# A linear-attention and gated-MLP kernel on one core: two heads of the attention share a pair of PSUM banks and one operation, and small vector work moves to GpSimd

## The chip, the cores and the metric

The kernel runs on one core of one Trainium2 chip. The metric is the device time of one execution in microseconds. Over three runs the kernel before took 1269.21 us at the median (1263.41 to 1276.26).

## The reference

What is computed is a linear attention over 8 batches, 8 heads, 576 tokens and a head size of 64, with 128 random features, and behind it a gated layer over the 4608 tokens (512 model columns, 1536 inner columns):

```python
def phi(x):                                   # x: q or k, already scaled by 64 ** -0.25
    proj = np.einsum('bhsd,md->bhsm', x, omega)
    sq = np.sum(x * x, axis=-1, keepdims=True) / 2.0
    h = proj - sq
    h = h - np.max(h, axis=-1, keepdims=True)
    return np.exp(h) / np.sqrt(m)
q_p, k_p = phi(q_s), phi(k_s)
kv = np.einsum('bhsm,bhsd->bhmd', k_p, v)
z = np.sum(k_p, axis=2)
out = einsum('bhsm,bhmd->bhsd', q_p, kv) / (einsum('bhsm,bhm->bhs', q_p, z)[..., None] + 1e-6)
x = out, heads side by side: (4608, 512)
gate = 1 / (1 + np.exp(-(x @ w_gate)))
return gate * (x @ w_val) @ w_out
```

The weights of the gated layer come in as 64-bit floats.

## The kernel before, in words

The attention works on "units" of two batches (1152 tokens, nine tiles of 128) and pairs of heads: four units `u`, four pairs `p`, two halves `b` (the two batches). It is written as generators, each a task that yields between its steps: `norms` (row sums of squares of q or k, line 489), `keys` (line 558, up to the tile `kv` of key features times values) and `queries` (line 601). `attention` (line 687) keeps up to six tasks going and steps them in turn.

The steps of one task are a chain through four engines. TensorE projects the tokens onto the features (`pp`, line 527 with each head's 64 rows of the array, in a bank per head, or line 536 for a tile that stands alone, with both heads in one matmul over 128 rows against a zero-padded omega). VectorE takes the maxima (`mx`, line 550), then the small tiles `hm` (line 554) and `nb` (line 573, keys) or `sub` (line 611, queries). For keys, ScalarE takes the exponentials `kp` out of the bank (line 582), and TensorE sums `pkv` (line 592). For queries, VectorE subtracts (`h`, line 617), TensorE transposes (`pt`, line 631), ScalarE takes the exponentials `qp` (line 633), TensorE multiplies with `kv` (`pn`, line 644), VectorE divides (`den`, `inv`, `x`, lines 649 to 654), TensorE transposes back (`px`, line 661), ScalarE copies (`xs`, line 667), and a DMA puts the rows into `xT` in DRAM. From the maxima on, each of these is done once per head.

The gated layer is in three passes. `first_pass` (line 224) makes four of the twelve column tiles from `xT`: products `gv` (line 243) in split single precision, a low and a high word of each operand, so three matmuls for each of four contraction steps, twelve per product. ScalarE takes the tanh of the gate (`ge`, line 264), VectorE multiplies (`ye`, line 271), and a DMA stores. The low words `xe` are subtracted on GpSimd (line 71). The first pass is interleaved with the attention: after each of its steps, `RATE` steps of the attention are recorded (lines 736 to 744), and since a chunk of tokens needs finished attention, `load` (line 215) records attention steps until they are there. `second_pass` (line 391, products `gw`, line 347) and `last` (line 440, products `po`, line 461) follow when the attention is done.

In between, the 64-bit weights are turned into single precision by `from_float64` (line 74): five VectorE operations and one more with the low word (line 94), then an addition on GpSimd (line 96) and subtractions there (line 177). Three of these conversions are left for the stretch after the attention (tiles `late`).

PSUM has eight banks: six with the tag `at` and two with `gv`. While the attention is alone, and again in the second and last pass, `any_bank` (line 124) deals all eight out in turn. While attention and first pass run together, the attention has the six and `gv` the two; after the attention, `gv` still has its two.

The order of the instructions on each engine isn't the order in which they are recorded. A scheduler sets it from its own costs of the operations and from when buffers come free; each engine then runs its list strictly in that order, and waits where an operand or a buffer isn't ready.

## Time and profile before

| what | value |
|---|---|
| median of three runs | 1269.21 us |
| profiled execution, its own time | 1265.23 us |
| its span, first to last instruction | 1263.4 us |
| first `gv` product on TensorE begins | 77.6 us |
| last `px` transpose of the attention begins | 521.9 us |
| first `gw` product of the second pass begins | 613.4 us |
| busy over the span: TensorE, VectorE, ScalarE, GpSimd | 94%, 67%, 38%, 34% |

The program has four stages: attention alone (to 77.5 us), attention with the first pass (to about 522 us), the rest of the first pass (to 613 us), then second and last pass. A view of the profile groups instructions by line, engine and operation: their busy time, the mean of one in ns, and what ended the idle time ahead of them. A busy time is the union of the spans in the group, and the spans of neighbouring matmuls overlap, so the pace of matmuls is read from the distance of their starts. A matmul of 32-bit floats shows as two records in the trace. "PEclk" is the clock granted to TensorE as a share of the full one.

### The profile page before, as it was taken

To read this page: it belongs to the slowest core of one execution; us is meant where nothing else is said; L and a number is where in the kernel's file an instruction comes from. 1 tells how busy PE (TensorE), PEld (TensorE's weight loads), DVE (VectorE), ACT (ScalarE), POOL (GpSimd) and SP (SyncE) were. 2 spreads that over 40 slices of the span, in tenths; PEclk is the share of its full clock that TensorE was granted. 3 is DMA by queue.
4 is the path that set the end of the run, shared out by engine and by line. 5 is a ranking of instruction groups with operands and counts; after the bars stand their busy time and mean duration, and the time that the engine had idled before them with its cause. 6 is when DMAs were issued, how large, how long until landed. Compare 5 with 4: busy or idle time off the path is not lost.

```text
span 1263.4 us, 23711 instructions
## 1 busy us (share of the span) xinstructions
PE 1189.8 (94%) x9052; PEld 1105.9 (88%) x9052; DVE 848.5 (67%) x1842; ACT 474.5 (38%) x971; POOL 431.3 (34%) x439
## 2 busy tenths in 40 slices
PE   7889899989899999987999999999999899999998
PEld 6778888777777887866899999999998899999998
DVE  4678788778847455475566565665668787677773
ACT  3445454534333434322422222322224443343331
POOL 0223041423422001163176666666666211111110
PEclk9679779989989999998999999999999999999999
DMA  7647577766673531456423333233328676666662
GB/s 241 208 159 241 187 239 255 253 212 211 219 244 107 164 97 57 139 206 235 148 88 122 147 125 115 95 122 122 134 85 285 208 223 190 208 193 185 196 186 93
DMA packets 100338, 219.40 MB, mean 174 GB/s; under 512 B 10624, under 2 KB 33408, under 8 KB 98432
## 3 DMA queue, kind: packets, MB, share of 16 engines
q1 hardware_dynamic: 87984, 198.94, 47.6%
q10 hardware_dynamic: 12240, 18.95, 4.2%
q8 instruction: 71, 1.16, 0.4%
q14 instruction: 43, 0.35, 0.1%
HBM read 141.82 MB, written 76.02 MB: 172 GB/s over the span
## 4 chain that ended last, share of the span: by engine, by line
PE 68%; DVE 11%; DMA 7%; issue 7%; POOL 4%; ACT 2%; SPq 1%; ACTq 0%; DVEq 0%; POOLq 0%
PE gw L347 25%; PE po L461 20%; PE gv L243 7%; PE pkv L592 6%; PE pn L644 4%; PE ppk L527 2%; PE pt L631 2%; POOL xe L71 2%; DMA xr<-xT 2%; PE ppq L527 1%; DVE mxk L550 1%; DMA u<-w 1%; DVE mxq L550 1%; DMA xT<-xs 1%; DVE h L617 1%
## 5 line engine op out<-in xcount | busy, mean ns | idle before, releaser
L347 PE MATMUL gw<-xl,u 128*128 128x256 f32 x3024 | 362.6, 282 | 6.1 <-DVE u L327 5.2
L347 PEld LDWEIGHTS gw<-xl,u 128*128 128x128 f32 x3024 | 361.1, 189 | 7.5 <-DVE u L327 6.0
L461 PE MATMUL po<-u,yh 128*128 128x256 f32 x1512 | 272.4, 283 | 0.0
L461 PEld LDWEIGHTS po<-u,yh 128*128 128x128 f32 x1512 | 234.8, 191 | 0.0
L461 PE MATMUL po<-u,yl 128*128 128x256 f32 x756 | 213.9, 283 | 4.0 <-DVE yl L71 4.0
L243 PE MATMUL gv<-xe,wh 128*128 128x512 f32 (+1 forms) x640 | 200.0, 392 | 2.9 <-POOL xe L71 2.8
L70 ACT ACTIVATE yh<-yr 128x896 fp32r<-128x896 f32 x108 | 100.3, 950 | 157.3 <-PE po L461 63.1
L461 PEld LDWEIGHTS po<-u,yl 128*128 128x128 f32 x756 | 144.3, 191 | 4.4 <-DVE yl L71 4.4
L243 PEld LDWEIGHTS gv<-xe,wh 128*128 128x128 f32 x640 | 120.6, 199 | 24.1 <-POOL xe L71 4.6
L243 PE MATMUL gv<-xe,wl 128*128 128x512 f32 (+1 forms) x320 | 128.3, 403 | 13.2 <-DVE ye L271 10.3
L71 DVE TENSOR_TENSOR yl<-yr,yh 128x896 fp32r<-128x896 f32 x91 | 101.1, 1123 | 37.0 <-PE po L461 23.1
L71 POOL TENSOR_TENSOR yl<-yr,yh 128x896 fp32r<-128x896 f32 x17 | 38.2, 2249 | 215.6 <-PE po L461 139.5
L71 POOL TENSOR_TENSOR xe<-xr,xe 128x512 fp32r<-128x512 f32 (+1 forms) x40 | 49.5, 1251 | 172.7 <-ACT xe L70 164.8
L592 PE MATMUL pkv<-v,kp 128*128 128x66 f32 x512 | 88.4, 308 | 13.9 <-ACT kp L582 13.8
L592 PEld LDWEIGHTS pkv<-v,kp 128*128 128x128 f32 x512 | 80.4, 222 | 22.6 <-ACT kp L582 19.2
L327 DVE TENSOR_TENSOR u<-gw,p 128x256 f32<-128x256 f32 x144 | 60.7, 422 | 58.7 <-PE gw L347 50.8
L243 PEld LDWEIGHTS gv<-xe,wl 128*128 128x128 f32 x320 | 63.7, 200 | 26.6 <-DVE ye L271 12.1
L96 POOL TENSOR_TENSOR c<-c 128x512 f32<-128x512 f32 x22 | 28.2, 1283 | 165.5 <-DVE c L94 91.0
L452 DVE TENSOR_TENSOR yr<-yr 128x128 f32<-128x128 f32 x144 | 64.4, 482 | 28.1 <-DMA yr<-ye 27.5
L644 PE MATMUL pn<-kv,qp 128*128 128x66 f32 (+1 forms) x640 | 75.5, 273 | 3.1 <-DVE h L617 3.1
L644 PEld LDWEIGHTS pn<-kv,qp 128*128 128x128 f32 (+1 forms) x640 | 70.4, 189 | 8.2 <-DVE h L617 3.5
L633 ACT ACTIVATE qp<-pt 128x512 f32<-128x512 f32 (+1 forms) x80 | 43.6, 555 | 89.1 <-PE pt L631 85.9
(106 smaller groups left out, 1776.9 us busy)
## 6 DMA issues: line engine op xcount, KB each, us to landing
yl<-yl SPq DMA_DIRECT2D x36, 896.0 KB, 3.8
yr<-yl SPq DMA_DIRECT2D x72, 448.0 KB, 4.0
xr<-xT SPq DMA_DIRECT2D x68, 256.0 KB, 4.4
c<-w SPq DMA_DIRECT2D x22, 512.0 KB, 4.9
w<-c SPq DMA_DIRECT2D x11, 1024.0 KB, 4.9
v<-va SPq DMA_DIRECT2D x32, 330.0 KB, 3.5
natk<-kn SPq DMA_DIRECT2D x36, 256.0 KB, 4.1
natq<-qn SPq DMA_DIRECT2D x36, 256.0 KB, 4.0
```

The costliest lines, as they stand in the source:

```text
L70: nc.scalar.activation(out=hi, in_=x, func=AF.Copy)
L71: (lo_engine or nc.vector).tensor_tensor(out=lo, in0=x, in1=hi.bitcast(F32), op=ALU.subtract)
L96: nc.gpsimd.tensor_tensor(out=x, in0=x, in1=r, op=ALU.add)
L243: nc.tensor.matmul(gv, lhsT=u[:, s], rhs=v, start=(m == 0), stop=(m == 3 * KC - 1))
L327: return nc.vector.tensor_tensor(out=o, in0=a, in1=b, op=ALU.add)
L347: nc.tensor.matmul(o, lhsT=u[:, k, s], rhs=v[:, kc, :], start=(first and m == 0), stop=(m == 5), skip_group_check=not first,)
L452: nc.vector.tensor_tensor(out=raw[:, o], in0=raw[:, a], in1=raw[:, b], op=op)
L461: nc.tensor.matmul(o, lhsT=u[:, i, :], rhs=v[:, k, :], start=(j + m == 0 and n in (1, 6, 5, 4)), stop=(j == NPAIR - 1 and m == 2), skip_gr ...
L527: nc.tensor.matmul(pps[h][:, i * M : (i + 1) * M], lhsT=raw[r, (t - t0) * P : (t - t0 + 1) * P], rhs=om_sb[r, h * M : (h + 1) * M], start= ...
L592: nc.tensor.matmul(pkv[:, h, :], lhsT=kp[b * MID + i, h], rhs=v[:, i, h, :], start=(i == 0), stop=(i == MID),)
L633: nc.scalar.activation(out=qp, in_=pt, func=AF.Exp)
L644: nc.tensor.matmul(pn[r, i, :], lhsT=qp[:, i, r], rhs=kvs[u, p, bb][:, h, :], start=True, stop=True,)
```

## The change

- Every projection takes both heads together: a tile of two banks `[128, 2, 512]`, head 0 in the first and head 1 in the second, and from there one operation for both heads: maxima, `h`, the exponentials of the queries, the division. The six `at` banks become three such pairs. The form with a zero-padded omega is gone; a tile that stood alone is now in a group with others (`GROUPS`: keys 0-2 and 3-4, then 5-8; queries 0-3, then 4-6 and 7-8).
- Omega is scaled once (`om_s`), so that `h` is an addition with `nb`. `hm` and `nb` are subtractions on GpSimd (lines 549 and 552 of the changed kernel).
- The squares come scaled from ScalarE, GpSimd adds the two halves of each head (`half`, line 510), and VectorE sums 32 values a head (line 511) in place of 64. The eight sums have buffers of their own.
- In `from_float64` the low word is scaled on ScalarE (line 94) and multiplied on GpSimd (line 95).
- The first chunk is 512 tokens, not two of 256, and the attention alone ends when 512 tokens are through (a group of queries makes 512 at once). `RATE` is 9 for 12, `FROM` 16 for 24; some buffer counts differ.
- After the attention, `gv` is dealt out over all eight banks. While the attention is alone, `pkv` and `px` take a `gv` bank, later one half of a pair.

The core of the diff:

```diff
-GROUPS = {"k": (((0, 1, 2, 3), (4,)), ((5, 6, 7, 8),)), "q": (((0, 1, 2, 3),), ((4,), (5, 6, 7, 8)))}
+GROUPS = {"k": (((0, 1, 2), (3, 4)), ((5, 6, 7, 8),)), "q": (((0, 1, 2, 3),), ((4, 5, 6), (7, 8)))}
...
-FROM = 24
+FROM = 16
...
-RATE = 12
-RAWS, KPS, VS, HS, XS = 6, 8, 3, 5, 3
+RATE = 9
+RAWS, KPS, VS, HS, XS = 6, 14, 3, 3, 2
...
-    nc.vector.scalar_tensor_tensor(out=r, in0=lo, scalar=2.0**-52, in1=r, op0=ALU.mult, op1=ALU.mult)
+    nc.scalar.activation(out=small, in_=lo, func=AF.Copy, scale=2.0**-52)
+    nc.gpsimd.tensor_tensor(out=r, in0=small, in1=r, op=ALU.mult)
     nc.gpsimd.tensor_tensor(out=x, in0=x, in1=r, op=ALU.add)
...
+    def two_banks(name):
+        return pairs.tile([P, 2, 512], F32, tag="at", bufs=3, name=name)
+    def one_bank(name):
+        return bank(name) if alone else two_banks(name)[:, 0]
...
-            gv = bank("gv", f"gv{o}_{j}_{i}")[:, :n]
+            gv = (any_bank if late else bank)(f"gv{o}_{j}_{i}")[:, :n]
...
-        chunks = [(0, Q), (Q, Q)] + [(c * NC, NC) for c in range(1, NCH)]
+        chunks = [(c * NC, NC) for c in range(NCH)]
...
-            nc.scalar.activation(out=x2, in_=x, func=AF.Square)
+            nc.scalar.activation(out=x2, in_=x, func=AF.Square, scale=SCALE / 2.0**0.5)
             yield
-            nc.vector.tensor_reduce(
-                out=s[:, t - t0, :], in_=x2.rearrange("p (h d) -> p h d", d=D), axis=AX.X, op=ALU.add
-            )
+            nc.gpsimd.tensor_tensor(out=half, in0=x2[:, :, 0], in1=x2[:, :, 1], op=ALU.add)
+            nc.vector.tensor_reduce(out=s[:, t - t0, :], in_=half, axis=AX.X, op=ALU.add)
...
-            nc.vector.scalar_tensor_tensor(
-                out=hm, in0=mx[:, i0:i1], scalar=SCALE, in1=s, op0=ALU.mult, op1=ALU.subtract,
-            )
+            nc.gpsimd.tensor_tensor(out=hm, in0=s, in1=mx, op=ALU.subtract)
+            nc.gpsimd.tensor_tensor(out=nb, in0=hm, in1=s, op=ALU.subtract)
...
-                nc.vector.scalar_tensor_tensor(
-                    out=h_sb,
-                    in0=pp,
-                    scalar=SCALE,
...
-                    op0=ALU.mult,
-                    op1=ALU.subtract,
-                )
+            nc.vector.tensor_tensor(
+                out=h_sb, in0=pp, in1=nb.unsqueeze(3).broadcast_to([P, 2, nt, M]), op=ALU.add
+            )
...
-            while not ready(Q):
+            while not ready(NC):
...
-                credit += RATE if n >= 4 * NE else RATE // 2
+                credit += RATE if n >= 2 * NE else RATE // 2
...
+        rest = ctx.enter_context(tc.tile_pool(name="rest", bufs=1, space=bass.MemoryType.PSUM))
+        cycle[:] = ["at", "at", "at", "gv"]
```

What it moves in the lists of the engines is seen at three places. The first is a group of keys, unit 1, pair 2, first half. Before, its maxima (`mxk1_2_0`) and both small tiles (`hmk1_2_0`, `nb1_2_0`) stand on VectorE:

```order
L550 TENSOR_REDUCE mxk1_2_0_1658<-ppk1_2_0_0_1659 128x4
L550 TENSOR_REDUCE mxk1_2_0_1658<-ppk1_2_0_1_1660 128x4
L550 TENSOR_REDUCE mxk1_2_0_1658<-ppk1_2_4_1671 128x2
L649 TENSOR_SCALAR den0_3_5_1_1703<-pn0_3_5_1_1698 128x4
L554 SCALAR_TENSOR_TENSOR hmk1_2_0_1674<-mxk1_2_0_1658,sqk1_0_1343 128x10
L503 TENSOR_SCALAR sqq2_0_3245<-ssq2_0_3038 128x32
L653 RECIPROCAL inv0_3_5_1_1705<-den0_3_5_1_1703 128x4
L573 SCALAR_TENSOR_TENSOR nb1_2_0_1678<-sqk1_0_1343,hmk1_2_0_1674 128x10
```

Now `hm` and `nb` of the same group stand in GpSimd's list. `c3` is a weight conversion, `halfq2_7` the squares of a later unit, `xe512` low words of the first pass:

```order
L510 TENSOR_TENSOR halfq2_7_3549<-x2q2_7_3519 128x256
L95 TENSOR_TENSOR c3_3528<-c3_3528 128x512
L96 TENSOR_TENSOR c3_3528<-c3_3528 128x512
L549 TENSOR_TENSOR hmk1_2_0_1536<-ssk1_0_1042,mxk1_2_0_1521 128x10
L552 TENSOR_TENSOR nbk1_2_0_1538<-hmk1_2_0_1536,ssk1_0_1042 128x10
L71 TENSOR_TENSOR xe512_2_1620<-xr512_0_904,xe512_2_1620 128x512
```

So the small tiles left a list of maxima and divisions and stand behind a multiplication and an addition of 128x512 that wait for the weights' DMA.

The second place is TensorE in a group of queries, unit 2, pairs 0 to 3. Before, each head's four transposes and products are pieces of their own:

```order
L631 MATMUL pt2_0_0_0_3356<-id_sb_69,h2_0_0_0_3311 128x128 x4
L631 MATMUL pt2_1_0_1_3368<-id_sb_69,h2_1_0_1_3269 128x128 x4
L631 MATMUL pt2_2_0_1_3375<-id_sb_69,h2_2_0_1_3291 128x128 x4
L631 MATMUL pt2_0_0_1_3382<-id_sb_69,h2_0_0_1_3313 128x128 x4
L527 MATMUL ppq2_3_0_0_3390<-om_sb_67,rawq2_3_0_3315 128x128
```

Now:

```order
L605 MATMUL pt2_0_0_3158<-id_sb_69,h2_0_0_3103 128x128 x8
L617 MATMUL pn2_1_0_3176<-kv2_1_0_2850,qp2_1_0_3132 128x66 x8
L539 MATMUL ppq2_2_0_3192<-om_s_71,rawq2_2_0_3084 128x128 x8
L617 MATMUL pn2_0_0_3208<-kv2_0_0_2732,qp2_0_0_3167 128x66 x8
L634 MATMUL px2_1_0_3232<-id_sb_69,x2_1_0_3189 128x128 x4
```

Both heads' eight go at once, and each of these rows fills one of the three pairs.

The third place is the end of the attention on TensorE. Before, the last `px` (unit 3, pair 3) stands among the products of the chunk from token 2560, and 319 matmuls `gv` are still to come:

```order
L644 MATMUL pn3_3_5_1_5726<-kv3_3_1_5299,qp3_3_5_1_5706 128x66 x4
L243 MATMUL gv2560_2_0_5868<-xe2560_3_5315,wh2_790 128x512
L243 MATMUL gv2560_2_1_5883<-xe2560_0_5306,wl2_791 128x512
L243 MATMUL gv2560_2_1_5883<-xe2560_0_5306,wh2_790 128x512 x2
L243 MATMUL gv2560_2_1_5883<-xe2560_1_5309,wl2_791 128x512
L243 MATMUL gv2560_2_1_5883<-xe2560_1_5309,wh2_790 128x512
L661 MATMUL px3_3_5_5736<-id_sb_69,x3_3_5_5645 128x128 x4
```

Now it stands among those of the chunk from token 3072, with 250 to come:

```order
L634 MATMUL px3_2_7_5494<-id_sb_69,x3_2_7_5481 128x128 x2
L252 MATMUL gv3072_3_0_5677<-xe3072_0_5304,wl3_891 128x512
L252 MATMUL gv3072_3_0_5677<-xe3072_0_5304,wh3_890 128x512
L634 MATMUL px3_3_7_5523<-id_sb_69,x3_3_7_5492 128x128 x2
L252 MATMUL gv3072_3_0_5677<-xe3072_0_5304,wh3_890 128x512
```

So 69 matmuls of 512 columns moved from behind the attention to within it.

More of the change, by code (lines that the diff above doesn't have):

```diff
@@ L111, in attn_glu_kernel @@
     yl = dram.tile([NPAIR - EP, P, NCH, 2, N_OPS, P], F32, name="yl")
-    om_sb = const.tile([P, 2 * M], F32, name="om_sb")
+    om_sb = const.tile([P, M], F32, name="om_sb")
     nc.sync.dma_start(out=om_sb, in_=om)
@@ L542, in projected @@
             i0, i1 = some[0][0] - t0, some[-1][-1] + 1 - t0
[L543 removed]
+            mx = pool.tile([P, 2, MID + 1], F32, tag="mx", bufs=4, name=f"mx{name}{u}_{p}_{some[0][0]}")[:, :, : i1 - i0]
             pps = []
             for tiles in some:
[L546 to L551 removed]
@@ new lines, in projected @@
+                for i, t in enumerate(tiles):
+                    for h in range(2):
+                        r = slice(h * D, (h + 1) * D)
+                        nc.tensor.matmul(
+                            pp[:, h, i], lhsT=raw[r, (t - t0) * P : (t - t0 + 1) * P], rhs=om_s[r],
+                            start=True, stop=True, skip_group_check=True,
+                        )
+                o = tiles[0] - t0 - i0
+                nc.vector.tensor_reduce(out=mx[:, :, o : o + nt], in_=pp, axis=AX.X, op=ALU.max)
@@ new lines, in queries @@
+            for h in range(2):
+                for i in range(nt):
+                    nc.tensor.transpose(out=pt[:, h, i], in_=h_sb[:, h, i], identity=id_sb)
+            qp = pool.tile([P, 2, nt, P], F32, tag="qp", bufs=HS, name=f"qp{id_}")
+            nc.scalar.activation(out=qp, in_=pt, func=AF.Exp)
+            yield
+            pn = two_banks(f"pn{id_}")[:, :, : nt * E].rearrange("p h (i e) -> p h i e", e=E)
+            for h in range(2):
+                for i, t in enumerate(tiles):
@@ L694, in attention @@
                     i for i, (name, needs, _) in enumerate(tasks[:AHEAD])
-                    if (ready(Q) or name[1] == name[-1] == 0) and done.issuperset(needs) and kinds.count(name[0][0]) < ACTIVE[name[0][0]]
+                    if (ready(NC) or name[1] == name[-1] == 0) and done.issuperset(needs) and kinds.count(name[0][0]) < ACTIVE[name[0][0]]
                 ]
@@ L715, in attn_glu_kernel @@
     late = None
+    alone = True
     stores = []
@@ L718, in attn_glu_kernel @@
         gates = first_pass()
-        with tc.tile_pool(name="a", bufs=1, side="right") as pool:
+        with (
+            tc.tile_pool(name="a", bufs=1, side="right") as pool,
+            tc.tile_pool(name="pairs", bufs=1, space=bass.MemoryType.PSUM) as pairs,
+        ):
             steps = attention(pool)
```

166 lines of the change are left out of this document (58 added, 108 removed).

## The prediction

> **What bounds the kernel now.** I read the page first: busy time per engine, and the clock granted to TensorE over 40 slices of the span.
>
> ```profile
> PE 1189.8 (94%) x9052; PEld 1105.9 (88%) x9052; DVE 848.5 (67%) x1842; ACT 474.5 (38%) x971; POOL 431.3 (34%) x439
> PEclk9679779989989999998999999999999999999999
> ```
>
> TensorE is busy 94% of the time and nothing else is above 67%. But its clock dips, all in the left half. So I took the busy times by stage, in stretches of the span (attention alone, attention with first pass, rest of the first pass, the two later passes). The columns are each engine's busy time, the granted clock, the DMA share and GB/s.
>
> ```profile
> 0.00:77.50 77.50, 60.85 (x358) 52.99 (x358) 47.29 (x117) 32.22 (x79) 10.55 (x13) 0.85 0.64 209
> 77.50:525.00 447.50, 418.04 (x3097) 360.05 (x3096) 317.30 (x820) 192.94 (x507) 106.87 (x103) 0.93 0.56 185
> 525.00:615.00 90.00, 77.32 (x323) 61.23 (x322) 49.70 (x67) 27.28 (x42) 37.43 (x32) 0.94 0.56 195
> 615.00:1263.40 648.40, 633.61 (x5280) 631.64 (x5278) 434.19 (x841) 222.07 (x344) 276.40 (x292) 1.00 0.48 158
> ```
>
> In the last row TensorE lacks 15 us of 648 and has its full clock. The change touches nothing there. The first 615 us hold what can be won: TensorE is idle for 77.5 - 60.9 = 16.7, 29.5 and 12.7 us, and a clock of 0.85, 0.93 and 0.94 costs about 11.6, 31.3 and 5.4 us more. Together that is 107 us of 615; some 508 are work at full clock. VectorE is busy 317 of 447.5 us in the middle, 71%. GpSimd, at 107, has room.
>
> The waits of TensorE say for what: the total, the number of times, and the longest. First in the middle stage, then (last row) behind the attention.
>
> ```profile
> PE pt L631 <- DVE h L617: 11.2, 13, 2.5
> PE pkv L592 <- ACT kp L582: 10.7, 10, 2.3
> PE pn L644 <- DVE h L617: 3.1, 1, 3.1
> PE gv L243 <- DVE ye L271: 10.3, 4, 5.4
> ```
>
> So 25.0 us of the 29.5 are the chain of an attention group being late, from VectorE directly or through the exponentials, and 10.3 of the 12.7 are a bank of `gv` that VectorE has not read yet.
>
> The clock isn't simply a matter of long waits. In this stretch TensorE sat still for 1.06 us of 10 and yet had half its clock:
>
> ```profile
> 150.00:160.00 10.00, 8.94 (x47) 8.31 (x48) 4.94 (x18) 2.45 (x4) 0.00 (x0) 0.50 0.29 85
> ```
>
> The Trainium skill's page "TensorE: Matmul & The Clock Gate" (Part 1) says that the clock halves after an idle window of about 3.4 us and returns after a busy one. This row disagrees: no wait of the middle stage is that long. By the rule the 31 us of lost clock there would not be, and fewer waits would bring nothing on that side; by the rows they are there. I count no gain in clock in the forecast.
>
> **The change, part by part.** *TensorE's own work.* 32 single tiles lose their both-heads matmul. Its place in the trace, start to start: 0.53 us at full clock, against 1.09 us for sixteen records of half-row matmuls.
>
> ```profile
> 136.32 1.16 PE L527 MATMUL ppk<-om_sb,rawk 64*128 64x128 f32 x16
> 137.41 0.70 PE L536 MATMUL ppk<-om_sb,rawk 128*128 128x256 f32 x2
> 137.94 1.04 PE L631 MATMUL pt<-id_sb,h 128*128 128x128 f32 x8
> ```
>
> 32 x 0.53 = 17.0 us go, and 64 half-row matmuls, two records each, come: 128 x 1.09/16 = 8.7 us. That saves 8.3 at full clock, double at half clock; I take 9. The first chunk's 192 matmuls of 256 columns become 96 of 512. Their pace is one low-word matmul to the next, three matmuls apart:
>
> ```profile
> 129.95 0.28 PE L243 MATMUL gv<-xe,wl 128*128 128x256 f32 x1
> 130.31 0.28 PE L243 MATMUL gv<-xe,wl 128*128 128x256 f32 x1
> 599.76 0.39 PE L243 MATMUL gv<-xe,wl 128*128 128x512 f32 x1
> 600.44 0.39 PE L243 MATMUL gv<-xe,wl 128*128 128x512 f32 x1
> ```
>
> 0.36/3 = 0.12 us and 0.68/3 = 0.227 us, so 23.0 becomes 21.8: 1 us. Sum: **-10** (-9 to -18).
>
> *The rest of the first pass.* It lasts from the last `px` to the first `gw`:
>
> ```profile
> 521.92 0.60 PE L661 MATMUL px<-id_sb,x 128*128 128x128 f32 x4
> 613.36 2.92 PE L347 MATMUL gw<-xl,u 128*128 128x256 f32 x23
> ```
>
> From 522.5 to 613.4 are 90.9 us, for 319 matmuls that need 319 x 0.227 = 72.4. The excess is 18.5. Afterwards 250 stand there, 56.8 us; the other 69 (15.7 us) are done earlier, which moves work and saves none. What saves is that `gv` gets eight banks, so four gates and values, 8 x 12 x 0.227 = 21.8 us of products, may lie between TensorE and a late `ye`. The longest wait in the row above is 5.4 us. I expect those 10.3 us to go. What is late next is the preparation of the second pass, since VectorE's 49.7 and GpSimd's 37.4 us of this stage now have 65 us in place of 91, and GpSimd gets the six multiplications of the late weights, 6 x 1.28 = 7.7 us. I keep 7.5 of the excess: **-11** (bounds -18.5 and 0, where the whole excess stays because VectorE is late everywhere).
>
> *VectorE's load.* One operation for both heads saves only the fixed part of an operation. The spans of the maxima and of `h` by size (shortest, median, longest) give it:
>
> ```profile
> L550 DVE TENSOR_REDUCE mxq<-ppq x80: 415/684/703, 34.3 to 513.1; 128x4 f32<-128x512 f32 x64, 128x2 f32<-128x256 f32 x16
> L617 DVE SCALAR_TENSOR_TENSOR h<-ppq,sub x80: 409/681/694, 40.9 to 515.7; 128x512 f32<-128x512 f32 x64, 128x256 f32<-128x256 f32 x16
> L653 DVE RECIPROCAL inv<-den 128x4 f32<-128x4 f32 (+1 forms) x80 | 13.0, 168 | 0.6
> L649 DVE TENSOR_SCALAR den<-pn 128x4 f32<-128x4 f32 (+1 forms) x80 | 12.7, 159 | 53.0 <-PE pn L644 52.3
> L611 DVE TENSOR_TENSOR sub<-sqq,hmq 128x8 f32<-128x8 f32 (+1 forms) x48 | 13.1, 274 | 0.2
> L554 DVE SCALAR_TENSOR_TENSOR hmq<-mxq,sqq 128x8 f32<-128x8 f32 (+1 forms) x48 | 10.0, 209 | 0.2
> L554 DVE SCALAR_TENSOR_TENSOR hmk<-mxk,sqk 128x10 f32<-128x10 f32 (+1 forms) x32 | 7.9, 251 | 0.3
> L573 DVE SCALAR_TENSOR_TENSOR nb<-sqk,hmk 128x10 f32<-128x10 f32 (+1 forms) x32 | 9.6, 303 | 0.2
> L499 DVE TENSOR_REDUCE ssq<-x2q 128x8 f32<-128x512 f32 x36 | 24.2, 679 | 0.5 <-ACT x2q L497 0.5
> L94 DVE SCALAR_TENSOR_TENSOR c<-c 128x512 f32<-128x512 uint32 x22 | 15.5, 703 | 0.3
> ```
>
> 256 elements take 0.415 us and 512 take 0.684: 1.05 ns an element and 0.146 us fixed. 160 maxima become 96 (48 groups of queries, 48 of keys), 64 x 0.146 = 9.3 us; `h` and `x` go from 80 to 48, 2 x 32 x 0.14 = 9.0; `den` and `inv` likewise, 32 x 0.327 = 10.5. `sub`, `hm` and `nb` leave: 13.1 + 10.0 + 7.9 + 9.6 = 40.6. The sums of squares lose 256 of 512 elements, 72 x 256 x 1.05 ns = 19.4. The low words leave: 36 x 0.703 = 25.3. Altogether 114 us, about 100 of them in the middle, where VectorE falls from 71% to 48%.
>
> *GpSimd's load.* It gets 72 halves of 256, 36 multiplications of 512 and 160 tiny subtractions. Nearest rows:
>
> ```profile
> L384 POOL TENSOR_TENSOR yl<-gl,yl 128x256 f32<-128x256 f32 x36 | 27.7, 770 | 2.2 <-DVE gl L382 2.2
> L96 POOL TENSOR_TENSOR c<-c 128x512 f32<-128x512 f32 x22 | 28.2, 1283 | 165.5 <-DVE c L94 91.0
> L874 POOL MEMSET const-float32-1.0<- 128x1 f32 x1 | 0.1, 98 | 0.0
> ```
>
> 0.770 and 1.283 us put 0.26 us at zero elements. No tiny subtraction is in the trace: it costs between the 0.098 of setting one element and the 0.770 of 256; I take 0.27, by the line through the two sizes. Then 72 x 0.77 + 36 x 1.28 + 160 x 0.27 = 145 us (117 to 225), some 125 in the middle: 107 becomes 232 of about 450 us, 52%. The multiplication reads its low word at a stride, which no GpSimd row shows; at worst twice the price, 46 us more. The page "GPSIMD Engine Reference" of the Trainium skill (section 4.1) speaks against this: elementwise work belongs on VectorE, GpSimd being about twice as slow. The rows agree, 1.283 against 0.703 us for neighbouring steps; but as an engine with time to spare pays, the sum doesn't change. ScalarE gets 36 copies of the size of this one, 36 x 0.634 = 23 us, at 193 busy of 447.5, and only GpSimd waits for them:
>
> ```profile
> L70 ACT ACTIVATE wh<-e 128x512 fp32r<-128x512 f32 x8 | 5.1, 634 | 10.2 <-POOL e L96 10.2
> ```
>
> There is a second cost. The same step of a weight conversion, in the middle and behind the attention, where GpSimd was busier (37.4 of 90 us):
>
> ```profile
> L85 DVE TENSOR_SCALAR c<-c 128x512 uint32<-128x512 uint32 x22 | 11.5, 523 | 0.2
> L85 DVE TENSOR_SCALAR late<-late 128x512 uint32<-128x512 uint32 x6 | 4.8, 821 | 0.1
> ```
>
> This step loses 0.30 us. If all five steps of the 30 conversions in the attention did, that would be 45 of the 100 us saved; VectorE still ends below 60%.
>
> *The waits of the middle.* The 25.0 us are a group's chain being late. Its VectorE part gets less queueing. Its GpSimd part is new: two dependent operations, 0.54 us, behind whatever stands ahead of them, in 80 groups. And the banks get scarcer: three pairs serve where six banks did, and a `pkv` or a `px` now takes a whole pair. I take the two as nearly even and count **-6** for waits, +-25.
>
> **The sum:** -10 - 11 - 6 = -27 us from the profiled execution's 1265.2 (its span of 1263.4 and 1.8 around it, which stay), so 1238. The median of the runs shown, 1269.2, is 0.3% above that execution; I forecast 1240.
>
> **Rivals.** *TensorE keeps its clock* (about 1210). If the groups' chains shorten as VectorE's load does, by a third or more, the waits fall to 12 us in place of 25, and of the 43 us of clock lost up to 525 us a third returns: -10 - 11 - 13 - 14 = -48, so 1217 from the profiled execution, or with the whole excess behind the attention gone 1209. For it: the half-clock stretches lie where groups are late. Against it: the row of 150 to 160, half clock with little idle time.
>
> *Nothing comes of VectorE's relief* (about 1262). It was at 71% and nobody's bound; GpSimd takes the place in the chain, and the eight banks only move the wait into the second pass's start. Then -10 from TensorE's work remain and some 7 us of new waits against them: 1265 - 10 + 7. For it: TensorE is at 93 to 94% already in the middle.
>
> *Slower: the small tiles stand behind the weights on GpSimd* (about 1290). GpSimd's list puts `hm` and `nb` of a group behind a multiplication and an addition of a conversion, which wait for the weights' DMA and five VectorE steps. Meanwhile a group of keys holds two of the three pairs, the other tasks share one, and TensorE, in order, stops at `pkv` or `pt`. There are 30 such conversion halves in the attention, 2 x 1.28 = 2.6 us each on GpSimd: 77 us if all is exposed. It decides from 0.9 us exposed per half (30 x 0.9 = 27); at two thirds, 51 us, the time is 1265 - 27 + 51 = 1289. The page "SBUF — State Buffer" of the Trainium skill (Who interferes with whom) adds that a GpSimd instruction and a VectorE one that needs their shared port block each other fully; the two rows of line 85 above agree with it (523 against 821 ns), and it would lengthen this chain further. Against it: `gv` products fill TensorE's list between the groups, and 0.9 us is more than the mean queue that 52% makes.
>
> **How the numbers follow.** The forecast, 1223 to 1256: 0.45. The clock kept, below 1223: 0.21. Nothing gained, 1256 to 1282: 0.17. Slower: 0.17. A change of 1%, 12.7 us, is about what a measurement can tell here. So faster 0.66, the same 0.17, slower 0.17. The range of 1205 to 1284 leaves out a little below and about a tenth above.
>
> **What would show it.** Right: the first `gw` starts near 587 us where it stood at 613; the wait of `gv` for `ye` is gone; VectorE in the middle is near 50% and GpSimd near 50%; TensorE's waits there are about 20 us, and some now name GpSimd or exponentials behind it. Wrong: if TensorE waits over 50 us in the middle for `kp` and `h` behind GpSimd's `nb`, the slower rival holds; if the tiny subtractions take over 0.5 us, my price of the chain was too low; if the clock row changes by much either way, I erred in leaving it out.

## The result, and the profile after

The changed kernel takes 1323.1 us at the median (four runs, 1319.24 to 1326.8) beside 1269.21 us for the kernel before in the same session: ratio 1.042 (95% interval 1.034 to 1.050). Some executions are in a slower state (one of the kernel before took 1864 us), and all medians and ratios here leave them out. The changed kernel is slower, by some 54 us. The prediction, 1240 us and most likely faster, was wrong.

The profiled execution took 1319.24 us, with a span of 1317.4. The page's busy times, and the clock over 40 slices:

```profile
PE 1212.5 (92%) x9020; PEld 1114.7 (85%) x9020; DVE 786.8 (60%) x1434; ACT 490.1 (37%) x968; POOL 564.0 (43%) x703
PEclk9988866998799999899979999999999999999999
```

VectorE lost 62 us of work, GpSimd gained 133, and TensorE, with 32 records fewer, is busy for longer. By stage, with the columns of the prediction's table (attention alone, attention with first pass, rest of the first pass, the later passes):

```profile
0.00:79.70 79.70, 62.75 (x353) 55.72 (x354) 40.92 (x69) 36.00 (x83) 34.39 (x50) 1.00 0.61 202
79.70:591.40 511.70, 451.56 (x3129) 374.91 (x3128) 264.19 (x466) 204.93 (x499) 211.45 (x328) 0.88 0.50 165
591.40:650.30 58.90, 57.75 (x249) 46.32 (x248) 35.31 (x42) 16.48 (x26) 38.06 (x32) 1.00 0.53 190
650.30:1317.40 667.10, 640.41 (x5293) 637.75 (x5291) 446.37 (x857) 232.70 (x360) 280.08 (x294) 0.98 0.48 161
```

The attention ends at 591 where it ended at 522.5. The moved `gv` work is 69 matmuls or 15.7 us of that, so about 53 us are lost ahead of it. In the middle TensorE is idle for 511.7 - 451.6 = 60.1 us, where it was 29.5, and its clock is 0.88 where it was 0.93. The rest of the first pass is 59 us in place of 91, but the last stage has grown by 17 us. Its first 50 us, in the kernel before and in the changed one:

```profile
613.40:663.40 50.00, 47.24 (x390) 46.63 (x389) 33.73 (x64) 19.11 (x33) 26.96 (x31) 1.00 0.39 137
```

```profile
650.30:700.30 50.00, 35.08 (x247) 33.99 (x246) 34.11 (x55) 24.44 (x38) 19.07 (x18) 0.76 0.61 210
```

247 matmuls fit in where 390 did. TensorE's waits over the whole span, the two longest rows and three of `gw` (total, number of times, longest):

```profile
PE pkv L580 <- ACT kp L571: 20.9, 10, 10.3
PE pt L605 <- DVE h L598: 20.8, 15, 5.8
PE gw L356 <- ACT xl L298: 8.1, 1, 8.1
...
PE gw L356 <- ACT p L367: 4.4, 1, 4.4
PE gw L356 <- DVE u L336: 4.1, 4, 1.4
```

Behind `kp` and `h` stands GpSimd. This is what ScalarE and VectorE waited for:

```profile
ACT kp L571 <- POOL nbk L552: 58.3, 23, 6.4
```

```profile
DVE h L598 <- POOL nbq L552: 30.1, 38, 4.2
```

One piece of the timeline shows how the lists hang together (ScalarE, GpSimd, VectorE and TensorE, start and duration; in brackets the idle time ahead and what ended it):

```profile
118.88 1.29 POOL L95 TENSOR_TENSOR c<-c 128x512 f32<-128x512 f32 x1 [1.75 <-DVE c L92]
120.13 0.72 POOL L510 TENSOR_TENSOR halfk<-x2k 128x256 f32<-128x256 f32 x1
120.80 1.26 POOL L96 TENSOR_TENSOR c<-c 128x512 f32<-128x512 f32 x1
...
122.70 3.13 POOL L186 TENSOR_TENSOR c<-c 128x256 f32<-128x256 f32 x4
...
125.79 0.71 POOL L510 TENSOR_TENSOR halfk<-x2k 128x256 f32<-128x256 f32 x1
...
126.54 0.42 DVE L511 TENSOR_REDUCE ssk<-halfk 128x8 f32<-128x256 f32 x1 [1.29 <-POOL halfk L510]
126.75 0.21 POOL L552 TENSOR_TENSOR nbk<-hmk,ssk 128x8 f32<-128x8 f32 x1
...
126.99 1.14 ACT L571 ACTIVATE kp<-ppk,nbk 128x128 f32<-128x128 f32 x4 [3.58 <-DVE ssk L511]
...
127.41 0.69 PE L580 MATMUL pkv<-v,kp 128*128 128x66 f32 x2 [10.29 <-ACT kp L571]
```

GpSimd works without a pause from 118.9 to 126.9, but on a conversion and on halves. VectorE's sum waits for a half that stands behind the conversion, `nb` comes at 126.75, and TensorE has stood still for 10.3 us. It looks like the prediction's slower rival. The experiments show that this is only part of it.

### The profile page after: what moved, and what is told of

The parts are those of the page before. It is cut to its first block, busy times and chain, and to the rows that moved or that the text cites. A ratio compares the mean times of both kernels' runs of the same rounds, so it can differ in the third digit from the quotient of the medians.

```text
span 1317.4 us, 23526 instructions
## 1 busy us (share of the span) xinstructions
PE 1212.5 (92%) x9020; PEld 1114.7 (85%) x9020; DVE 786.8 (60%) x1434; ACT 490.1 (37%) x968; POOL 564.0 (43%) x703
## 4 chain that ended last, share of the span: by engine, by line
PE 45%; DVE 3%; DMA 1%; issue 1%; SPq 0%; POOL 0%; ACT 0%; DVEq 0%; ACTq 0%; POOLq 0%
PE gw L356 26%; PE po L470 19%; DMA u<-w 1%; DVE u L221 1%; DMA yr<-ye 1%; DVE yr L461 0%; DVE yl L71 0%; SPq L443 0%; POOL late L186 0%; DVE u L336 0%; DVE o L336 0%; DVE ye L280 0%; DVE yl L336 0%; DVE u L215 0%; DVE gl L336 0%
## 5 line engine op out<-in xcount | busy, mean ns | idle before, releaser
L356 PE MATMUL gw<-xl,u 128*128 128x256 f32 x3024 | 367.6, 284 | 18.2 <-ACT xl L298 8.1
L252 PE MATMUL gv<-xe,wh 128*128 128x512 f32 x576 | 199.0, 421 | 3.2 <-POOL xe L71 3.1
L252 PEld LDWEIGHTS gv<-xe,wh 128*128 128x128 f32 x576 | 112.5, 200 | 27.9 <-POOL xe L71 5.6
L252 PE MATMUL gv<-xe,wl 128*128 128x512 f32 x288 | 124.3, 434 | 9.0 <-ACT xe L70 6.2
L571 ACT ACTIVATE kp<-ppk,nbk 128x128 f32<-128x128 f32 x256 | 69.4, 387 | 61.9 <-POOL nbk L552 58.3
L617 PEld LDWEIGHTS pn<-kv,qp 128*128 128x128 f32 (+1 forms) x640 | 77.4, 199 | 17.2 <-issue 5.7
L617 PE MATMUL pn<-kv,qp 128*128 128x66 f32 (+1 forms) x640 | 85.2, 292 | 6.6 <-DVE x L627 3.1
L544 DVE TENSOR_REDUCE mxk<-ppk 128x6 f32<-128x768 f32 (+2 forms) x48 | 44.7, 952 | 60.4 <-PE ppk L539 60.1
L252 PEld LDWEIGHTS gv<-xe,wl 128*128 128x128 f32 x288 | 57.0, 199 | 21.0 <-ACT xe L70 6.4
L71 POOL TENSOR_TENSOR xe<-xr,xe 128x512 fp32r<-128x512 f32 x36 | 48.3, 1350 | 58.6 <-ACT xe L70 58.6
```

The costliest lines, as they stand in the source:

```text
L71: (lo_engine or nc.vector).tensor_tensor(out=lo, in0=x, in1=hi.bitcast(F32), op=ALU.subtract)
L252: nc.tensor.matmul(gv, lhsT=u[:, s], rhs=v, start=(m == 0), stop=(m == 3 * KC - 1))
L356: nc.tensor.matmul(o, lhsT=u[:, k, s], rhs=v[:, kc, :], start=(first and m == 0), stop=(m == 5), skip_group_check=not first,)
L544: nc.vector.tensor_reduce(out=mx[:, :, o : o + nt], in_=pp, axis=AX.X, op=ALU.max)
L571: nc.scalar.activation(out=kp[t][:, h], in_=pp[:, h, i], func=AF.Exp, bias=nb[:, h, o + i : o + i + 1],)
L617: nc.tensor.matmul(pn[r, h, i], lhsT=qp[:, h, i, r], rhs=kvs[u, p, bb][:, h, :], start=True, stop=True,)
```

## Experiments

"Before" is always the kernel before in the same session (medians 1266 to 1270 us). Two theories stood at the start: G, that GpSimd's new work is the loss, and P, that the three pairs in place of six banks are.

**The three pieces of GpSimd's work, taken back one by one.** `e1`, `e2` and `e3` each give one piece of the changed kernel back to VectorE, `e4` all three:

```diff
e1 -nc.gpsimd.tensor_tensor(out=half, in0=x2[:, :, 0], in1=x2[:, :, 1], op=ALU.add)
e1 -nc.vector.tensor_reduce(out=s[:, t - t0, :], in_=half, axis=AX.X, op=ALU.add)
e1 +nc.vector.tensor_reduce(out=s[:, t - t0, :], in_=x2.rearrange("p (h d) -> p h d", d=D), axis=AX.X, op=ALU.add)
e2 -nc.scalar.activation(out=small, in_=lo, func=AF.Copy, scale=2.0**-52)
e2 -nc.gpsimd.tensor_tensor(out=r, in0=small, in1=r, op=ALU.mult)
e2 +nc.vector.scalar_tensor_tensor(out=r, in0=lo, scalar=2.0**-52, in1=r, op0=ALU.mult, op1=ALU.mult)
e3 -nc.gpsimd.tensor_tensor(out=hm, in0=s, in1=mx, op=ALU.subtract)
e3 -nc.gpsimd.tensor_tensor(out=nb, in0=hm, in1=s, op=ALU.subtract)
e3 +nc.vector.tensor_tensor(out=hm, in0=s, in1=mx, op=ALU.subtract)
e3 +nc.vector.tensor_tensor(out=nb, in0=hm, in1=s, op=ALU.subtract)
```

> The changed kernel with the sums of squares on VectorE alone (64 values a head, no halves on GpSimd). Theory G: GpSimd loses 55 us of work, and VectorE's list no longer waits for it in the sums; about 1285. Theory P: 1315 or more.

> The changed kernel with the weights' low words multiplied on VectorE as before. Theory G: GpSimd loses 46 us of work, ScalarE 24; about 1295, and the stretch after the attention and the start of the second pass get their share. Theory P: 1315 or more.

> The changed kernel with the two small subtractions per group on VectorE. Theory G, in the form that the small tiles stand behind halves and conversions in GpSimd's list: ScalarE's 58 us and VectorE's 30 us of waits for nb go, TensorE's waits for kp and h halve, about 1285. If instead it is VectorE's maxima that are late, since their list waits for GpSimd's halves: 1310 or more. Theory P: 1315 or more.

> The changed kernel with all its new GpSimd work taken back to VectorE (sums of squares over 64 values, the low words' multiplication, the two small subtractions); the pairs of banks, the grouping, the first chunk and the late banks stay. Theory G (GpSimd's list is what TensorE waits for in the first 360 us): TensorE's idle time between its first gv and 360 us falls from 54 us to below 30 and the time to about 1255 (1240 to 1275). Theory P (three pairs in place of six banks are what it waits for): it stays at 1305 or more, the waits for kp and h unchanged in sum.

| kernel | us | ratio to before | 95% interval |
|---|---|---|---|
| changed | 1323.1 | 1.042 | 1.034 to 1.050 |
| e1, squares on VectorE | 1298.1 | 1.024 | 1.018 to 1.031 |
| e2, low words on VectorE | 1311.8 | 1.035 | 1.028 to 1.042 |
| e3, small tiles on VectorE | 1305.2 | 1.029 | 1.023 to 1.036 |
| e4, all three | 1281.3 | 1.012 | 1.004 to 1.021 |

Of 4.2% above before, 3.0% or 38 us go with the three pieces. One at a time they give back 1.8, 0.7 and 1.3%, some 3.9% in sum, more than together, though the intervals are wide; the squares aren't clearly apart from the small tiles, nor the low words alone from the changed kernel. All four times lie above theory G's figures and below theory P's. GpSimd's work is most of the loss. But `e4` still isn't faster than before, though it has the pairs, the shorter TensorE work and the eight late banks. Its middle stage says where the two parts lie:

```profile
83.40:554.30 470.90, 433.56 (x3124) 361.72 (x3123) 304.42 (x625) 189.84 (x474) 104.25 (x98) 0.92 0.54 177
```

The attention ends at 554 us. Of the 53 us that the changed kernel lost ahead of that point some 36 are gone; some 17 are still lost with GpSimd's old load.

**The eight late banks alone**, on the kernel before:

```diff
-            gv = bank("gv", f"gv{o}_{j}_{i}")[:, :n]
+            gv = (any_bank if late else lambda name: bank("gv", name))(f"gv{o}_{j}_{i}")[:, :n]
```

(and `cycle[:] = ["at", "at", "at", "gv"]` set when the pool `late` opens).

> The kernel before with one part of the change alone: after attention's end gv goes round all eight banks; attention, its six banks and its order stay as they were. Theory 'eight banks pay' (the prediction's Part 2): about 11 us faster than before, ratio about 0.991; the stretch from the last px to the end, 741 us in the kernel before, comes to about 730. Theory S, 'the second pass is not ready sooner': in the trace of the changed kernel the rest of the first pass is 32 us shorter (16 of it gv work moved ahead of it), and the first 50 us of the second pass hold 247 gw matmuls where they held 390, with TensorE waiting for high and low parts of xT and of the weights; so what the banks gain at gv is waited for at the first gw. By S the time is within 4 us of before, ratio 0.997 to 1.003, the stretch 741 within 5, and the first 50 us of gw hold clearly fewer than 390 matmuls.

1262.5 us, ratio 0.996 (0.993 to 1.000): about 5 us, half of the forecast. The rest of the first pass fell from 91 to 79 us, and the second pass began like this:

```profile
525.10:604.30 79.20, 76.53 (x324) 60.86 (x323) 43.92 (x56) 22.81 (x35) 38.04 (x30) 0.98 0.61 214
604.30:654.30 50.00, 44.10 (x332) 43.28 (x331) 37.20 (x67) 22.64 (x39) 24.84 (x27) 0.90 0.40 144
```

332 matmuls where before had 390, and the clock is 0.90 in place of 1.00: part of the 12 us is lost there. These are waits between 520 and 670 us:

```profile
ACT u L211 <- DMA u<-w: 26.0, 7, 20.3
PE gw L347 <- ACT xl L289: 2.8, 1, 2.8
PE gw L347 <- DVE xl L292: 1.6, 1, 1.6
```

ScalarE stands 20.3 us for one of the second pass's weights (`u`), and behind it in its list are the parts of `xT` (`xl`) for which TensorE then waits. `e12` was to give the second pass its operands sooner: `N_TAIL` is 2, one conversion moves into the attention, and three units of weights are loaded at the start of the rest in place of two.

```diff
-N_TAIL = 3
+N_TAIL = 2
-                started = [unit(late, n) for n in range(2)]
+                started = [unit(late, n) for n in range(3)]
```

> The kernel before with the eight late banks (1262.5 us), and besides one of the three weight conversions of the rest of the first pass done within attention (N_TAIL 2), so that a third unit of the second pass's weights can be loaded and split from the start of that rest. Theory S, 'the second pass is not ready sooner': with less to convert and load in that stretch more of what the eight banks gain at gv is kept: the first 50 us of gw hold more than the 332 matmuls they hold with the banks alone, and the time is 3 to 7 us less, 1255 to 1260. Rival, 'what starts late is xT and the first two units, not the third': no gain, or the added conversion costs attention up to 5 us: 1262 to 1268.

```profile
611.30:661.30 50.00, 48.19 (x398) 47.56 (x397) 34.41 (x66) 19.62 (x34) 27.66 (x31) 1.00 0.38 139
```

398 matmuls: the start of the second pass is as good as before. That fits weights that came late, but it isn't isolated: the second pass also begins 7 us later than in `e5`, so everything it needs had more time. And the time is 1262.5 us again (0.997, 0.994 to 1.000). The last `px` stood at 534.1 us in place of 525.1: what the second pass won, the attention paid, with one more conversion in it. Nothing is gained.

**GpSimd's work without the pairs.** `e6` puts the three pieces on GpSimd in the kernel before, with its six banks by head.

> The kernel before, six banks by head and order as they were, with the three pieces of work that the change puts on GpSimd (half sums of squares, the two subtractions behind the maxima, the low words' product with ScalarE's copy ahead of it; the scale goes into omega as in the change). Theory G, 'GpSimd's list stands in the chain, whatever the banks': putting the three back on VectorE took 42 us from the changed kernel's time, 36 of it before the last px, so here they cost about as much: 36 us, 26 to 46, ratio 1.021 to 1.036, and ScalarE's kp and VectorE's h wait for nb by tens of us. Rival, 'only together with the pairs': with six banks by head a late nb holds one bank of six and not a pair of three, so the cost is 15 us or less, ratio 1.012 at most.

1306.5 us, ratio 1.030 (1.027 to 1.034), 38 us. The loss comes about without the pairs, and in the same size; the rival that it needs them falls.

**What remains with the pairs.** Three variants of `e4`: `e7` cuts the first chunk in halves again (`chunks = [(0, Q), (Q, Q)] + ...`, `ready(Q)`, `FROM = 24`); `e8` puts `pkv` and `px` in `gv`'s banks throughout (`one_bank` returns `bank(name)`); `e9` makes `h` and `qp` by head, inside the pairs:

```diff
-            nc.vector.tensor_tensor(out=h_sb, in0=pp, in1=nb.unsqueeze(3).broadcast_to([P, 2, nt, M]), op=ALU.add)
+            for h in range(2):
+                nc.vector.tensor_tensor(out=h_sb[:, h], in0=pp[:, h], in1=nb[:, h].unsqueeze(2).broadcast_to([P, nt, M]), op=ALU.add)
```

> The changed kernel with all three pieces back on VectorE (1281 us, first gw at 614 us, last px at 554 us where before had 522), and besides with the first chunk in two halves of 256 tokens as before, its gates starting after 256 tokens of attention, with four times NE steps at the lower rate. Theory O, 'the order costs what is left': with pairs alone the last px comes 16 us later than before, beyond the gv moved ahead of it, since the gates start later and at another rate; by it 10 to 16 us go, 1265 to 1271. Theory B, 'three pairs are scarcer than six banks': the order has no part, 1276 to 1286.

> The changed kernel with all three pieces back on VectorE (1281 us), and besides with pkv and px, which need one bank each, in gv's two banks throughout, as they are before the gates start, so that they hold no pair. Theory B, 'three pairs are scarcer than six banks': a pkv or px that takes a whole pair for a single bank leaves two pairs for pp, pt and pn; without that TensorE's idle time between first gv and last px falls from 37 us to 27 or less and the time to 1265 to 1273. Theory O, 'the order costs what is left': within 5 us of 1281, or above it, since gv then waits for the copies of pkv and px to free its banks.

> The changed kernel with all three pieces back on VectorE (1281 us), and besides with h and qp again by head: two h of 512 columns where one of 1024 stood, and an exp for each head's transposes. Pairs of banks, maxima and the rest stay. Neither the order (1278) nor pkv and px (1301) explained the 12 us that pairs alone leave. Theory L, 'an operation twice as long starts the next step later': TensorE's transposes of the first head need not wait for the second's h, so waits of pt for h (10 us in that kernel) halve and the time comes to 1268 to 1276. Theory B, 'a pair is freed for both heads at once': the banks are held as long as before, the two shorter operations only cost VectorE and ScalarE their overhead again, and the time stays at 1281 or rises to 1290.

1278.4 us (1.009, 1.006 to 1.012), 1300.6 us (1.022, 1.017 to 1.027) and 1284.4 us (1.014, 1.010 to 1.018), beside `e4`'s 1281.3 (1.012). None of the three changes takes the remaining 1% away: `e7` and `e9` aren't clearly apart from `e4`, and in `e8` the attention ends at 577.6 us in place of 554.3. What the pairs cost by themselves stays open.

**Does a list wait too early?** `e10` puts VectorE's sum one step behind its half in the changed kernel (`RATE` 10), `e11` does so on the kernel with late banks (`RATE` 13):

```diff
             nc.gpsimd.tensor_tensor(out=half, in0=x2[:, :, 0], in1=x2[:, :, 1], op=ALU.add)
-            nc.vector.tensor_reduce(out=s[:, t - t0, :], in_=half, axis=AX.X, op=ALU.add)
+            if t > t0:
+                nc.vector.tensor_reduce(out=s[:, t - 1 - t0, :], in_=last_half, axis=AX.X, op=ALU.add)
+            last_half = half
```

> The changed kernel (1320 us) with all of its GpSimd work, but VectorE's sum over a half is put one step of its task behind the half, when the next half is issued; RATE is 10 for 9 so that as much gv as in the changed kernel is left at attention's end (258 of 249). Putting the squares wholly on VectorE gave back 22 us. Theory G1, 'the sums hold VectorE's list up': a sum that stands right behind its half makes the maxima behind it wait for GpSimd; with the half long done these waits go while GpSimd's load stays, and 10 to 20 us come back: 1298 to 1310, with VectorE's waits for halves under 5 us. Theory G2, 'GpSimd's own list is too long': the halves stand ahead of hm and nb as before, so the time stays at 1315 to 1325.

> The kernel before with the eight late banks (1262.5 us), and besides the squares' half sums on GpSimd with VectorE's sum one step later and the scale in ScalarE's squares; maxima, subtractions and low words stay on VectorE; RATE is 13 for 12 so that as much gv is left at attention's end. By G1 (a piece of work on GpSimd costs nothing if no list waits for it) VectorE loses about 27 us of work and 3 to 8 us are won: 1254 to 1260. By G2 (GpSimd's list is too long) its 72 halves of 0.77 us delay the parts of xT and of the weights, and the time is 1265 to 1280.

1350.7 us (1.066, 1.061 to 1.071) and 1278.9 us (1.009, 1.006 to 1.013): both slower than the kernels that they start from, and G1, that only the wait matters, fails twice; `e10` is slower than G2 allowed, too. `e14` and `e15` have the same lag and the same `RATE`, with whole sums on VectorE (`in_=last_x2`, 64 columns a head) and three buffers for the squares in place of two.

> The kernel with late banks and lagged halves (1279 us) in the same order and with the same RATE, but with the sums of squares wholly on VectorE (all 64 columns of a head), still one step later. It tells whether the 16 us above the late banks alone (1262.5 us) come from GpSimd's halves or from the order. By G1 or G2 (the halves): 1260 to 1268. By 'the order alone' (sums a step later, RATE 13): 1274 to 1284.

> The changed kernel with sums one step later (1351 us) in the same order and with RATE 10, but with the sums of squares wholly on VectorE. With the sums where the change has them, moving the squares to VectorE gave 1298 us. By 'the halves' it comes back to near that, 1295 to 1310; by 'the order alone' (a sum that comes later holds up the tasks that need it, and RATE 10) it stays at 1325 to 1345.

`e14` takes 1257.7 us (0.994, 0.989 to 0.998), `e15` 1329.4 us (1.049, 1.043 to 1.054). So on the kernel with late banks, halves on GpSimd cost 1.6% or some 20 us even where nothing waits for them at once. In the changed kernel they cost 1.7%, and the other order a good deal as well: `e15` stands 2.5% above `e1`, which differs only in the lag, `RATE` and the squares' third buffer.

**Load or result?** Four variants of the kernel before. `e13` gives GpSimd operations of the right sizes on a tile of ones that nobody reads; `e16` the small subtractions, unread, beside VectorE's own; `e17` halves and products at their true places, unread; `e18` the small subtractions alone, read as in the change (with omega and the squares scaled as there).

```diff
e13 +    idle_work["n"] = lambda w: nc.gpsimd.tensor_tensor(out=unread[:, :w], in0=unread[:, :w], in1=unread[:, :w], op=ALU.mult)
e16 +            nc.gpsimd.tensor_tensor(out=dhm, in0=s, in1=mx[:, i0:i1], op=ALU.subtract)
e16 +            nc.gpsimd.tensor_tensor(out=dnb, in0=dhm, in1=s, op=ALU.subtract)
e17 +            nc.gpsimd.tensor_tensor(out=half, in0=both[:, :, 0], in1=both[:, :, 1], op=ALU.add)
e17 +    for o in (0, 256): nc.gpsimd.tensor_tensor(out=made, in0=x[:, o : o + 256], in1=x[:, o : o + 256], op=ALU.mult)
e18 +            nc.gpsimd.tensor_tensor(out=hm, in0=s, in1=mx[:, i0:i1], op=ALU.subtract)
e18 +            nc.gpsimd.tensor_tensor(out=nb, in0=hm, in1=s, op=ALU.subtract)
```

> The kernel before, with GpSimd given operations of the sizes and number of the change's (256 columns for each half, 512 for each low word, two of 8 for each group) that read and write one tile of ones that nobody else uses: the load without the results. The kernel before with the real work took 38 us more. Theory G1, 'the results stand in the chain': nobody waits for these, so the time is within 8 us of before, 1260 to 1276. Theory G2, 'a fuller GpSimd delays what it had before, and VectorE beside it': at least half of the 38 us, 1285 to 1306.

> The kernel before with the change's two small subtractions on GpSimd for each group besides its own on VectorE: GpSimd's list has to wait for VectorE's maxima 80 times, and nobody reads what it makes. If a part of the cost is that GpSimd's list, standing at a maximum that is late, delays its own older work (xe, the additions of the conversions), the time is 8 us or more above before, 1275 to 1290; if the cost is in the group's chain alone (G1), it is within 6 us of before, 1261 to 1273.

> The kernel before with the change's halves on GpSimd besides VectorE's full sums, and with two products of 256 for each low word, at the times and places of the real ones (they read the squares and the words that the real ones read), and nobody reads what they make. ScalarE's next squares still wait for a half that reads their buffer, and the conversion's addition stands behind the product. Theory G1, 'results that are waited for are the price': within 10 us of before, 1260 to 1279. Theory G2, 'the load itself': at least half of the 38 us that the real work cost there, 1286 to 1306; the conversion steps on VectorE are then longer than before by 0.1 us or more, as in the changed kernel.

> The kernel before with the two subtractions behind the maxima on GpSimd, read by ScalarE's kp and VectorE's h as in the change (the scale in omega and in the squares); squares and low words stay on VectorE. Unread and besides VectorE's own, the same subtractions cost nothing (1269.3 us against 1269.5). Theory G1: now the chain of each group goes through GpSimd's list, and putting them back on VectorE gave 17 us in the changed kernel: 8 to 20 us, 1275 to 1289. Theory G2 (only a full list costs): with 107 us of other work on GpSimd in the middle nothing is ahead of them, and VectorE's list is 30 us shorter, so 1258 to 1272.

| kernel | us | ratio to before | 95% interval |
|---|---|---|---|
| e13, idle load | 1320.0 | 1.040 | 1.036 to 1.044 |
| e16, subtractions, unread | 1269.3 | 1.001 | 0.998 to 1.004 |
| e17, halves and products, unread | 1299.9 | 1.023 | 1.017 to 1.029 |
| e18, subtractions, read | 1271.1 | 1.000 | 0.996 to 1.003 |

`e13` doesn't answer the question, and its time lies outside what either theory gave. Its operations wait for nothing, so the scheduler put most of them in front. GpSimd is busy 96 of the first 113 us, and the first `gv` starts at 112.6 us in place of 77.6:

```profile
0.00:112.60 112.60, 68.96 (x359) 59.93 (x359) 56.15 (x121) 31.73 (x79) 96.47 (x219) 0.71 0.43 141
```

`e17` goes further. Its lists are those of the kernel before: the same 9052 records of TensorE and 969 operations of ScalarE in the same order, VectorE's 1842 with two neighbours exchanged, and GpSimd's old 439 in their order with 144 new ones between. Nobody reads the new results, and VectorE is relieved of nothing. It loses 29 us. The whole time up to the first `gw`, in the kernel before, in `e16` and in `e17`:

```profile
0.00:613.40 613.40, 554.61 (x3761) 472.66 (x3762) 413.26 (x1000) 252.06 (x626) 154.85 (x147) 0.92 0.57 190
```

```profile
0.00:614.80 614.80, 558.13 (x3760) 475.96 (x3761) 409.76 (x1000) 252.42 (x626) 193.75 (x307) 0.92 0.57 190
```

```profile
0.00:648.00 648.00, 575.47 (x3761) 490.59 (x3762) 426.48 (x1000) 252.10 (x626) 262.50 (x291) 0.89 0.54 180
```

Read the counts first: they are the same on TensorE, VectorE and ScalarE. With 108 us more on GpSimd, VectorE's 1000 instructions take 13.2 us longer. TensorE's 3761 matmuls take 20.9 us longer, at a clock of 0.89 in place of 0.92, and TensorE's idle time grows from 58.8 to 72.5 us. The last two together are the 34.6 us of this execution. In `e16` GpSimd has 39 us more, in small pieces, and VectorE isn't slowed. The waits that grew most in `e17` are those for `kp` in the attention and for `ye` behind it (10.7 and 10.3 us in the prediction's rows):

```profile
PE pkv L603 <- ACT kp L593: 15.9, 11, 3.2
PE gv L251 <- DVE ye L279: 14.1, 4, 5.8
```

Two limits of this test. The share of the clock rests on one execution of each kernel. Over its whole span this one of `e17` has a clock of 0.944, the profiled one of the kernel before 0.960. But in the session of `e17` the kernel before ran at 0.938 to 0.967 (median 0.947) and `e17` at 0.927 to 0.950 (median 0.9465), and an execution of the kernel before at 0.944 took 1269.9 us. So the time is clearly apart, and how much of it is the clock isn't shown. And two links to GpSimd's list are left in `e17`: a conversion's old addition stands behind the unread products, and the halves hold the squares' buffers. VectorE's conversions waited 17.4 us for such additions up to the first `gw` where they had waited 10.3, and ScalarE's squares 2.4 us for halves. The 29 us are the price of the load with these links.

Most of VectorE's 13.2 us are in the six conversion steps. The low words' multiplication (line 94 of the kernel before, 703 ns in the prediction's row) is the one that grew most, while the sums of squares (679 ns there) did not grow:

```profile
L97 DVE SCALAR_TENSOR_TENSOR c<-c 128x512 f32<-128x512 uint32 x22 | 18.7, 848 | 0.3
...
L510 DVE TENSOR_REDUCE ssq<-x2q 128x8 f32<-128x512 f32 x36 | 24.1, 675 | 4.6 <-ACT x2q L505 4.6
```

The Trainium skill's page "SBUF — State Buffer" (Who interferes with whom) says that a VectorE instruction with two inputs in SBUF contends with GpSimd's reads, and a reduction never does. These two rows agree. But another step with two such inputs didn't grow, 795 to 770 ns (first the kernel before, then `e17`):

```profile
L88 DVE SCALAR_TENSOR_TENSOR c<-c 128x512 uint32<-128x512 uint32 x22 | 17.5, 795 | 0.2
```

```profile
L91 DVE SCALAR_TENSOR_TENSOR c<-c 128x512 uint32<-128x512 uint32 x22 | 16.9, 770 | 0.2
```

And the four steps with one such input grew by 6 us together. A single step also moves without any of this: line 81 took 452 ns before and 586 in `e16`, where VectorE as a whole isn't slower. So the two rows don't show that this is the mechanism.

`e18` shows the other half: with the small tiles in every group's chain through GpSimd, but the rest of its list as before, nothing is lost, though nothing is won by VectorE's shorter list either. They cost 17 us in the changed kernel (`e3`). The piece of the timeline above suggests that what stands ahead of them there is the reason; no run isolates it.

## Why the prediction was wrong

**The step that failed** is the one on the waits of the middle: "I take the two as nearly even and count -6 for waits, +-25." Up to the last `px` the kernel lost some 53 us where -16 was forecast (the -10 of TensorE's own work and this -6). I set VectorE's shorter queue against two GpSimd operations of 0.54 us together and fewer banks. The runs show a third term that I had left out of the sum: large work on GpSimd has a price beyond the small tiles' way through its list, 29 us for halves and products that nobody reads (`e17`), and 38 us net for the whole with the results read (`e6`). Of the 53 us, some 36 go when the three pieces leave GpSimd (`e4`); the other 17 are still lost with the pairs, and their cause stays open. I had a row that pointed to the third term, the conversion step of 523 ns that took 821 behind the attention, but charged it only against VectorE's saving.

**TensorE's own work, -10.** Its size was not isolated: the counts came out (32 records fewer, as -64 + 128 - 96 gives), but `e4`, which keeps this saving, is 1.2% slower than before.

**The rest of the first pass, -11.** In that stage the step was right: `gv`'s wait for `ye` fell from 10.3 us to

```profile
PE gv L252 <- DVE ye L280: 0.7, 1, 0.7
```

and the stage took 59 us for 64 forecast. But I closed the sum at the first `gw`. From the end of the last `px`, at 522.5 us, to the end were 740.9 us with 72.4 of `gv` in them, 668.5 without; now they are 726.0 from 591.4, with 56.8, and 669.2 without. Nothing is left. The rival "nothing comes of VectorE's relief" had said so: the banks move the wait into the second pass's start. On the kernel before they bring 5 us (`e5`).

**VectorE's load, -114.** It fell by 62. The operations for both heads are as cheap as forecast: their groups have 1024, 768 and 512 columns, 768 on average, for which the prediction's line gives 0.146 + 768 x 0.00105 = 0.952 us, and `h` takes 0.955 (the row below). The five conversion steps that stayed on VectorE grew by 22 us, from 103 to 125. The rest of the gap is my sum: it added up spans, and the spans of neighbouring VectorE operations overlap. In the kernel before some 944 us of spans make 848.5 us of busy time, so what left the list frees less than its spans. The middle stands at 264.2 of 511.7 us, 52%, for 48% forecast.

```profile
L598 DVE TENSOR_TENSOR h<-ppq,nbq 128x1024 f32<-128x1024 f32 (+2 forms) x48 | 45.8, 955 | 30.4 <-POOL nbq L552 30.1
```

**GpSimd's load, 145 us.** It is 133, and my prices were good: a small subtraction takes 0.20 to 0.24 us (0.27 forecast), a half 0.77, a product 1.31, hardly more for the stride than the addition next to it (1.28 us):

```profile
L95 POOL TENSOR_TENSOR c<-c 128x512 f32<-128x512 f32 x22 | 28.7, 1306 | 37.4 <-DVE c L92 14.6 <-DVE inv L625 8.5 <-ACT c L94 7.3
L510 POOL TENSOR_TENSOR halfk<-x2k 128x256 f32<-128x256 f32 x36 | 27.5, 768 | 23.8 <-ACT x2k L506 21.0 <-DVE ssk L511 1.4 <-DVE den L621 1.1
L549 POOL TENSOR_TENSOR hmq<-ssq,mxq 128x8 f32<-128x8 f32 (+2 forms) x48 | 11.5, 241 | 115.0 <-DVE mxq L544 114.9
L552 POOL TENSOR_TENSOR nbq<-hmq,ssq 128x8 f32<-128x8 f32 (+2 forms) x48 | 9.7, 203 | 3.7
```

A good price per operation and a good load said nothing of what the load does to the others.

**The clock.** "I count no gain in clock in the forecast" left out a possible loss as well: in the middle the changed kernel had 0.88 where it was 0.93. In the profiled execution of `e17` 20.9 of 34.6 us are the same matmuls at a lower clock. Over the whole span the changed kernel's four executions had 0.910 to 0.944 and `e17`'s 0.927 to 0.950, the kernel before 0.938 to 0.975 over all sessions of the experiments. So the clock is lower with the change, but it varies by itself, and how many us it costs isn't shown.

**The slower rival** had the right sign and named the right engine, at 0.17. It gave 1290 us, and the kernel took 33 more. Its mechanism, small tiles behind the weights' work, was only part of it: the tiles alone cost nothing (`e18`), and the weights' and squares' work costs without them (`e17`).

What stays open: what the pairs cost (`e4` and its variants), how the 13 us of VectorE, the waits, the clock and the two links to GpSimd's list in `e17` follow from one another, and how much of `e10`'s loss is the order. The best kernel of the study is `e14`, late banks with whole sums one step later, at 1257.7 us: 0.6% faster than before (0.2 to 1.1%), not clearly apart from the late banks alone.

## What to carry to other kernels

Work that moves to an engine with time to spare isn't free for that reason alone: run it first as unread load at its true place, with all other lists as they were, and see what it costs there. Compare several executions, since the clock of a single one can mislead. A stage that is made shorter must be followed into the next one, whose loads may have needed the time. And load for such a test has to depend on real operands, or the scheduler moves it to where it measures something else.

## What was not expected of the hardware

The same 1000 VectorE instructions, two neighbours exchanged, took 3.2% longer beside 108 us more of GpSimd work in operations of 256 columns (`e17`), and not longer beside 39 us more of it in operations of at most 10 (`e16`). TensorE's granted clock in these executions was 0.89 beside 0.92, with only 13.7 us of added idle time in 648; that this comes with the load, and not with the execution, isn't shown.
